# The last gelu of batch 1 ahead of the copies of batch 0's output, and T4's sums made beside batch 1's first product and stored

## The chip, the cores and the metric

The kernel runs on one core of one Trainium2 chip. The metric is device time in microseconds (us) of one execution; lower is better. A core has a matrix engine (PE, with its weight loads shown apart as PEld), a vector engine (DVE), a scalar engine for activations and copies (ACT), GpSimd (POOL, all but unused here) and a queue that issues the transfers between chip memory and HBM (SP). Each engine works through its own list of instructions in order, and waits where an instruction needs what another engine has not yet delivered.

## The reference

Eight batches, eight heads, 512 tokens and 32 states of width 64. Attention runs both ways between tokens and states; the 544 rows per batch then go through a two-layer network with the quick gelu.

```python
scores = scale * x @ state.T;   a  = softmax(scores);   xread = a  @ state      # 512 x 64 per head
scores2 = scale * state @ x.T;  a2 = softmax(scores2);  sread = a2 @ x          #  32 x 64 per head
y = concatenate([xread, sread], axis=2)          # rows of 512 features, heads side by side
h = y @ w_in                                     # 512 -> 2048
g = h * (1.0 / (1.0 + exp(-1.702 * h)))
return g @ w_out                                 # 2048 -> 512
```

All of it is in fp32.

## The kernel before, in words

**Tiles and batches.** The 512 tokens of a batch are four chunks of 128. The first product of the network is folded with the attention: for each batch, `att_M` multiplies the states with `w_in` (the tiles M), and the "up" product multiplies M with the transposed attention weights `aT`. Its gelu is written into tiles `g`, two of the 16 hidden chunks per tile. The second product, "down", multiplies the `g` tiles with `w_out`.

**Batches 0 and 1.** Batch 0 is done plainly: `up_x` (L529; its products are at L524, its gelu on ACT at L527) and `down` (L542), which adds the 16 hidden chunks into four PSUM banks, `bank_o[0]` to `bank_o[3]`, one for each chunk of tokens. The loop over f (from L1227 on) does one hidden chunk of batch 0's down product per step, and in its odd steps one of the last eight up products of batch 1, from the list `rest`. In the last step, f = 15, `down` also copies each bank into `osb` (L549, on ACT) and sends it out (L550, on SP); `osb` is one buffer, so each copy waits until the transfer of the one before has landed. In the source the last up product of batch 1 comes after these four copies, so its gelu stands behind them on ACT.

**Strassen.** From batch 1 on, products are done by Strassen's scheme (seven products in place of eight). The down product is `strassen_two`: the outer products P1 and P2 are plain (L745); the others, called P5, P6, P3, P7 and P4 in that order, are each done by a second level of seven small products, `strassen_low` (matmuls at L696; PSUM is gathered by DVE at L701 and copied by ACT at L705 and L711). The additions that prepare the left factors are DVE instructions (L752, of 0.68 us for 128x512). The right factors are sums of blocks of `w_out`, made once, around the end of the f loop: `T1`, `T2` and `T4` lie in `sums`, `T3` in `w_out`. Each of them needs three more sums for the inner level (`low_sums`, three subtractions of 128x512), and `low_third` (one subtraction in place). `low_made` puts the three sums in the tile `low`; `low_away` puts them in a room with the tag `xT` and stores them to HBM (`low_keep`, L648); later they are loaded from there (`low_load`, L645). The tag `xT` has one buffer: the next to use it is the exponentials of the next batch, `att_s_exp` (L372), which must wait until the store has read the room.

**T4.** Its sums are made in batch 1 by `low4_make`, as an entry of the hook `run`, between P3 and P7. They are written into the room with the tag `xn`, where batch 2's x lies until `att_sread` (L500 on PE) has read it. From batch 2 on `low4_load` (L666) loads them from HBM at the same place in the order. P4 is the first to read them.

**Order.** There is no scheduler: the order in the source is the order on each engine. What runs beside the products hangs on named hooks: "P1a" is called after the first half of P1, "P5.3" after the third small product of P5, "run" between P3 and P7. `hooks_next` fills them with the attention of the next batch. For batch 1 the entry "P1a" holds the last preparations of the right factors.

The end of the loop, where the change is made:

```python
        if f % 2 == 1:
            up_x(1, rest.pop(0))
        ...
        if f == NF - 1:
            for u in range(NU - 1):
                s3(1, u, S)
            T_of(B12, B22, B12)
            low_away(3, T3)
            low_third(T3)
            turn_x(2)
            low_made(2, T2, 0)
    s12(1, NU - 1, S)
    s3(1, NU - 1, S)
```

`s12` (L565, L566) and `s3` (L571) make left factors from the `g` tiles; the call for the last tile, `NU - 1`, needs the gelu of the last up product. `turn_x(2)` (L156) is four transposes, `low_made(2, T2, 0)` three subtractions into `low[:, 0:3]`, of which batch 1's `aT` is the first two thirds until the last up product has read it.

Of the kernel before, what the change touches and what calls it, by code (L numbers as in the profile page):

```python
# [20 lines left out]
def kernel(  # L21
# [39 lines left out]
    NF = DF // P  # L61
# [42 lines left out]
    T1, T2, T4 = (sums[:, i].rearrange("p (f n) -> p f n", f=HF) for i in range(3))  # L104
# [47 lines left out]
    def turn_x(b):  # L152

        A[b]["xT"] = xsq[b]
        for j in range(NPR):
            nc.vector.transpose(xsq[b][:, j], xsq[b][:, j])  # L156
# [36 lines left out]
    for i, v in enumerate((8.0 * most, 8.0 * (most - least))):  # L193
        t = konst.tile([P, 1], FP32, name=f"edge_{i}")
# [33 lines left out]
    def round_b(i, ahead, follows):  # L228


        if i not in begun:
            fraction(i)
        dst = begun.pop(i)
        lo, hi = words(i)
        sc = power.pop(i)
        nc.vector.scalar_tensor_tensor(sc, hi, -0x80000000, sc, ALU.bitwise_and, ALU.bitwise_or)
        powers_to(ahead)

        nc.vector.scalar_tensor_tensor(dst, lo, 2.0**-32, dst.bitcast(I32), ALU.mult, ALU.add)
        del raw[i]  # L240
        if follows and i + 1 in raw:
            fraction(i + 1)
        nc.vector.scalar_tensor_tensor(dst, dst, 2.0**-20, sc.bitcast(FP32), ALU.mult, ALU.mult)
# [3 lines left out]
    def before(i):  # L247

        nin = NFC * NPR
        return i - (nin - NPR if i < nin else 2 * NPR if i < nin + NPR else NPR)  # L250

    def load_weights(upto):
        while done["load"] < min(upto, len(PIECES)):
            load_weight(done["load"])
            done["load"] += 1

    def powers_to(n):
        while done["a"] < min(n, len(PIECES)):
            load_weights(done["a"] + 1)
            round_a(done["a"])  # L260
            done["a"] += 1

    def round_to(n, ahead=AHEAD):

        nin = NFC * NPR
        while done["b"] < min(n, len(PIECES)):
            i = done["b"]
            powers_to(i + 1)
            round_b(i, min(i + 1 + ahead, max(nin, i + 1)), i + 1 < nin and (i + 1 < n or i >= NPR))
            done["b"] += 1  # L270
            while done["b"] > NPR and done["load"] < len(PIECES) and before(done["load"]) < done["b"]:
                load_weights(done["load"] + 1)
# [209 lines left out]
    def att_eT(b, g):  # L482

        a = A[b]
        if g == 0:
            a["eT"] = apool.tile([P, NG, SCH, P], FP32, tag="eT", name=f"eT_{b}")
        ps = att_ps([P, SCH, P], f"eT_{b}_{g}")
        for c in range(SCH):
            nc.tensor.transpose(ps[:, c], a["e2"][g][0][:, P * c : P * (c + 1)], ident)
        nc.scalar.copy(a["eT"][:, g], ps)  # L490
# [29 lines left out]
    def up(key, f, ntok, lhs, rhs, spare=False):  # L520
        hps = att_ps([P, ntok], f"h_{key}_{f}") if spare else psH.tile([P, ntok], FP32, tag="h", name=f"h_{key}_{f}")
        n = len(lhs)
        for i in range(n):
            nc.tensor.matmul(hps, lhs[i], rhs[i], start=(i == 0), stop=(i == n - 1))  # L524
        if f % 2 == 0:
            G[key, f // 2] = free.pop(0)
        nc.scalar.activation(out=G[key, f // 2][:, f % 2, :ntok], in_=hps, func=AF.Gelu_apprx_sigmoid)  # L527

    def up_x(b, f, spare=False):  # L529
        c, o = divmod(P * f, FC)  # L530
        m = A[b]["M", c]
        up(b, f, S, [m[:, g, o : o + P] for g in range(NG)], [A[b]["aT"][:, g] for g in range(NG)], spare)
# [3 lines left out]
    def down(key, r, fs, dst, last):  # L536

        if fs[0] == 0:
            O[key, r] = bank_o[r]
        ops = O[key, r]  # L540
        for f in fs:
            nc.tensor.matmul(  # L542
                ops, G[key, f // 2][:, f % 2, P * r : P * (r + 1)], w_out[:, f], start=(f == 0), stop=(f == NF - 1)
            )
            if last and f < HF and f % 2:
                free.append(G.pop((key, f // 2)))
        if fs[-1] == NF - 1:
            osb = opool.tile([P, DM], FP32, tag="osb", name=f"osb_{key}_{r}")
            nc.scalar.copy(osb, ops)  # L549
            nc.sync.dma_start(dst, osb)  # L550
# [96 lines left out]
    def low_keep(k, src):  # L647
        nc.sync.dma_start(outside[k], src)  # L648

    def low4_room():  # L650
        t = xpool.tile([P, SCH, H, D], FP32, tag="xn", name="low4")
        return t.rearrange("p c h d -> p (c h d)")[:, : 3 * FC]

    def low_parts(t):
        return [t[:, FC * k : FC * (k + 1)].rearrange("p (f n) -> p f n", f=QF) for k in range(3)]

    def low4_make(a):
        t = low4_room()
        for fn, args in low_sums(T4, low_parts(t)):
            fn(*args)  # L660
        low_keep(4, t)
        a["low4"] = t

    def low4_load(a):
        a["low4"] = low4_room()
        nc.sync.dma_start(a["low4"], outside[4])  # L666
# [6 lines left out]
    def halves_of(t):  # L673

        return [t[:, QF * i : QF * (i + 1), P * k : P * (k + 1)] for i in range(2) for k in range(2)]

    def low_sums(t, rooms):

        b11, b12, b21, b22 = halves_of(t)
        t1, t2, t4 = rooms  # L680
        return [(T_of, v) for v in ((t1, b12, b11), (t2, b22, t1), (t4, b21, t2))]

    def low_third(t):
        _, b12, _, b22 = halves_of(t)
        T_of(b12, b22, b12)
# [441 lines left out]
    def rounds(n):  # L1127
        round_to(done["b"] + n)
# [78 lines left out]
    B11, B12, B21, B22 = (w_out[:, HF * i : HF * (i + 1), HN * k : HN * (k + 1)] for i in range(2) for k in range(2))  # L1207

    def T_of(t, x0, x1):
        nc.vector.tensor_tensor(out=t, in0=x0, in1=x1, op=ALU.subtract)  # L1210
# [15 lines left out]
    rest = list(range(2 * nper, NF))  # L1226
    for f in range(NF):  # L1227
        rounds(1)
        round_to(NFC * NPR + f + 1)
        for r in range(SCH):  # L1230
            down(0, r, [f], out_x[0, r], r == SCH - 1)
        if f in (0, 2):
            for g in range(NG):
                att_eT(f // 2, g)
        if f in (0, nper * 2):
            att_M(1, 2 + f // (nper * 2))
        if f in (1, 3):
            att_sread(f // 2)
        if f in (2, 4):
            att_srT(f // 2 - 1)  # L1240
        if f % 2 == 1:
            up_x(1, rest.pop(0))
        if f == HF:
            load_state(2)
            load_x_squares(2)
        if f == NF - 2:
            T_of(T1, B12, B11)
            low_away(6, B22)
            low_made(5, T1, 1)
            for u in range(NU - 1):  # L1250
                s12(1, u, S)
            T_of(T2, B22, T1)
            low_third(T1)
        if f == NF - 1:
            for u in range(NU - 1):
                s3(1, u, S)
            T_of(B12, B22, B12)
            low_away(3, T3)
            low_third(T3)
            turn_x(2)  # L1260
            low_made(2, T2, 0)
    s12(1, NU - 1, S)
# [5 lines left out]
    for b in range(1, B):  # L1268
        if b > 1:
            ahead = {"P1a": [(up_strassen(b, S, *parts_x(b), A[b]["sums"]), ())]}  # L1270
        else:
            ahead = {"P1a": [(low_third, (B22,)), (T_of, (T4, B21, T2)), (low_third, (T2,))], "P7.7": [(low_third, (T4,))]}
        if b + 1 < B:
            if b > 1:
                turn_x(b + 1)
            hooks = hooks_next(b + 1)
        else:

            steps, left, right = sr_sums()
            order = (  # L1280
                ("P5.6", 2), ("P6.1", 3), ("P6.3", 6), ("P6.4", 7), ("P7.5", 8), ("P7.6", 9), ("P4.1", 16, 17), ("P4.5", 18, 19),
            )
            hooks = {name: [steps[i] for i in n] for name, *n in order}
            hooks["P3.7"] = [(low_third, (T1,))]
            beside = steps[10:16] + [(low_third, (t,)) for t in (T2, T3, T4, B22)]
            ahead["P1a"][:0] = [steps[i] for i in (0, 1, 4, 5)]
        for name, first in ahead.items():
            hooks[name] = first + hooks.get(name, [])
        a4 = {}

        at = hooks.setdefault("run", [])
        k = 3 if b + 1 < B else 0
        at[k:k] = [(low4_load if b > 1 else low4_make, (a4,))]
        strassen_two(b, out_of(b), hooks, a4)
        if b + 2 < B:
            load_state(b + 2)
            load_x_squares(b + 2)
# [35 lines left out]
```

## Time and profile before

Three runs took 713.96, 714.00 and 714.05 us. The profiled execution is one of 713.74 us, of which the engines' span is 712.0 us; its granted PE clock is 0.998.

| engine | busy us | share of the span | instructions |
|---|---|---|---|
| PE | 697.9 | 98% | 4973 |
| DVE | 602.0 | 85% | 1246 |
| ACT | 231.2 | 32% | 456 |
| POOL | 0.8 | 0% | 8 |

The transfers moved 77.1 MB, 108 GB/s over the span. Shares of busy time are means over stages with different limits. What a change in one stage is worth is read from that stage's timeline and waits: which engine stands still, and for whom. In the trace the stage around the change runs from about 144 us (the f loop's last two steps) to 209.4 us (the first up product of batch 2); batch 2's same stage, from P1 on, ends at 285.1 us.

### The profile page before, as it was taken

To read this page: it belongs to the slowest core of one execution; us is meant where nothing else is said; L and a number is where in the kernel's file an instruction comes from. 1 tells how busy PE (TensorE), PEld (TensorE's weight loads), DVE (VectorE), ACT (ScalarE), POOL (GpSimd) and SP (SyncE) were. 2 spreads that over 40 slices of the span, in tenths; PEclk is the share of its full clock that TensorE was granted. 3 is DMA by queue.
4 is the path that set the end of the run, shared out by engine and by line. 5 is a ranking of instruction groups with operands and counts; after the bars stand their busy time and mean duration, and the time that the engine had idled before them with its cause. 6 is when DMAs were issued, how large, how long until landed. Compare 5 with 4: busy or idle time off the path is not lost.

```text
span 712.0 us, 12663 instructions
## 1 busy us (share of the span) xinstructions
PE 697.9 (98%) x4973; PEld 557.9 (78%) x4975; DVE 602.0 (85%) x1246; ACT 231.2 (32%) x456; POOL 0.8 (0%) x8
## 2 busy tenths in 40 slices
PE   8989999999999999999999999999999999999996
PEld 3433444457888799888998899879987998899995
DVE  6999899969988999789968997899789997888650
ACT  5686511023214322433233322441343224300210
POOL 0000000000000000000000000000000000000000
PEclk9999999999999999999999999999999999999999
DMA  8921246217633184408550674138431940031001
GB/s 234 363 78 53 95 150 138 115 45 188 190 128 61 34 202 144 87 0 182 164 118 1 117 202 119 29 71 192 141 60 34 203 145 22 0 114 66 16 1 29
DMA packets 143770, 77.10 MB, mean 108 GB/s; under 512 B 113888, under 2 KB 127712, under 8 KB 143712
## 3 DMA queue, kind: packets, MB, share of 16 engines
q1 hardware_dynamic: 143712, 76.31, 41.1%
q8 instruction: 39, 0.64, 0.4%
q14 instruction: 19, 0.16, 0.1%
HBM read 60.29 MB, written 15.99 MB: 107 GB/s over the span
## 4 chain that ended last, share of the span: by engine, by line
PE 93%; ACT 2%; DVE 2%; DMA 2%; SPq 0%; issue 0%; DVEq 0%; ACTq 0%
PE low L696 21%; PE o L1058 17%; PE o L745 14%; PE o L696 10%; PE o L542 8%; PE h L524 7%; PE upx L1058 6%; PE M L320 4%; PE o L585 2%; PE o L320 1%; PE sr L500 1%; PE warm L125 1%; PE upx_sr L1058 1%; DMA out_dram<-osb_sr 1%; DMA xn<-in_x_dram 1%; DVE g L752 1%
## 5 line engine op out<-in xcount | busy, mean ns | idle before, releaser
L1068 DVE TENSOR_TENSOR g<-o,g 128x512 f32<-128x512 f32 (+1 forms) x140 | 88.0, 650 | 51.1 <-PE o L1058 50.2
L745 PE MATMUL o<-w_out,g 128*128 128x256 f32 x448 | 100.5, 380 | 0.0
L745 PEld LDWEIGHTS o<-w_out,g 128*128 128x128 f32 x448 | 84.2, 190 | 16.9 <-issue 5.5
L1065 ACT ACTIVATE g<-g 128x512 f32<-128x512 f32 (+1 forms) x84 | 49.8, 600 | 100.8 <-DVE g L1068 100.8
L1058 PE MATMUL upx<-aT,M 128*128 128x256 f32 x192 | 49.3, 379 | 0.0
L1058 PE MATMUL o<-ta,M 128*128 128x256 f32 x192 | 49.3, 379 | 0.0
L1058 PE MATMUL o<-ta,ms 128*128 128x256 f32 x192 | 48.3, 379 | 0.0
L696 PE MATMUL low<-low,g 128*128 128x128 f32 x336 | 44.4, 275 | 0.0
L460 ACT COPY M<-M 128x512 f32<-128x512 f32 x64 | 33.2, 596 | 28.1 <-PE M L320 28.1
L696 PEld LDWEIGHTS low<-low,g 128*128 128x128 f32 x336 | 40.9, 192 | 0.0
L1058 PEld LDWEIGHTS o<-ta,ms 128*128 128x128 f32 x192 | 36.5, 190 | 5.0
L1058 PEld LDWEIGHTS o<-ta,M 128*128 128x128 f32 x192 | 36.5, 190 | 5.0
L1058 PEld LDWEIGHTS upx<-aT,M 128*128 128x128 f32 x192 | 36.0, 190 | 4.7
L696 PE MATMUL low<-sums,later 128*128 128x128 f32 x280 | 37.1, 275 | 0.0
L696 PEld LDWEIGHTS low<-sums,later 128*128 128x128 f32 x280 | 34.6, 192 | 0.5 <-ACT pu L705 0.2
L320 PE MATMUL M<-w_in,stT 64*32 64x512 f32 x512 | 32.7, 594 | 0.2 <-ACT eT L490 0.2
L524 PE MATMUL h<-low,M 128*128 128x512 f32 x64 | 29.8, 600 | 1.4 <-DVE low L408 1.4
L696 PE MATMUL low<-w_out,g 128*128 128x128 f32 x224 | 29.7, 275 | 0.9 <-DVE pu L701 0.9
L524 PE MATMUL h<-aT,M 128*128 128x512 f32 x64 | 28.7, 599 | 1.4 <-ACT M L460 1.4
L542 PE MATMUL o<-w_out,g 128*128 128x512 f32 x64 | 28.7, 594 | 0.0
L542 PE MATMUL o<-w_out,sums 128*128 128x512 f32 x64 | 28.4, 594 | 0.0
L696 PEld LDWEIGHTS low<-w_out,g 128*128 128x128 f32 x224 | 27.3, 192 | 1.1 <-DVE pu L701 1.1
(208 smaller groups left out, 1282.2 us busy)
## 6 DMA issues: line engine op xcount, KB each, us to landing
low<-low SPq DMA_DIRECT2D x78, 256.0 KB, 3.6
later<-in_moe_w_out_dram SPq DMA_DIRECT2D x16, 512.0 KB, 3.4
xn<-in_x_dram SPq DMA_DIRECT2D x28, 256.0 KB, 4.8
low<-low SPq DMA_DIRECT2D x9, 768.0 KB, 4.6
w_out<-in_moe_w_in_dram SPq DMA_DIRECT2D x12, 512.0 KB
xsq<-in_x_dram SPq DMA_DIRECT2D x96, 64.0 KB, 2.3
out_dram<-osb SPq DMA_DIRECT2D x18, 256.0 KB, 3.0
out_dram<-later SPq DMA_DIRECT2D x14, 256.0 KB, 2.2
```

What stands on the lines that cost most here:

```text
L125: nc.tensor.matmul(ps, zeros[:, :P], zeros, start=True, stop=True)
L320: nc.tensor.matmul(ps[g][st], A[b]["stT"][rows, st], rhs(rows, j), start=True, stop=True)
L460: nc.scalar.copy(m[:, g], ps[g])
L500: nc.tensor.matmul(ps[st, g], a["eT"][:, g, c, st], xn[b][:, c, NG * j + g], start=(c == 0), stop=(c == SCH - 1),)
L524: nc.tensor.matmul(hps, lhs[i], rhs[i], start=(i == 0), stop=(i == n - 1))
L542: nc.tensor.matmul(ops, G[key, f // 2][:, f % 2, P * r : P * (r + 1)], w_out[:, f], start=(f == 0), stop=(f == NF - 1))
L585: nc.tensor.matmul(ps[:, r], lhs[f][:, P * r : P * (r + 1)], rhs[:, f], start=(first and r == 0 and f == 0), stop=(f == HF - 1), skip_grou ...
L696: nc.tensor.matmul(ps, lhs[f], rhs[:, f], start=(first and f == 0), stop=(f == QF - 1), skip_group_check=True)
L745: nc.tensor.matmul(ps[:, r], lhs[f][:, P * r : P * (r + 1)], rhs[:, f], start=(r == 0 and f == 0), stop=(f == HF - 1), skip_group_check=True,)
L1058: nc.tensor.matmul(ps[:, k], lhs[i][:, o : o + P], rhs[i], start=(first and k == 0 and i == 0), stop=(i == n - 1), skip_group_check=True,)
L1065: nc.scalar.activation(out=dst, in_=src, func=AF.Gelu_apprx_sigmoid)
L1068: nc.vector.tensor_tensor(out=dst, in0=ps, in1=x, op=ALU.add)
```

## The change

Three things, all around the seam between batch 0 and batch 1:

1. The last up product of batch 1 comes at the head of step f = 15, ahead of batch 0's last down products, their copies and their output transfers.
2. The preparations with `s3`, `T3` and its `low_away` move from step 15 into step 14, ahead of the output transfers in the source. On DVE the order of these instructions stays what it was; on SP the store of T3's sums now stands ahead of the four output transfers.
3. `low4_make` goes away. T4's three sums are made by `low_away(4, T4)` in the hook "P1a" of batch 1, in the `xT` room, and are stored; `low_third(T4)` follows them there, and leaves "P7.7". In "run" batch 1 now loads the sums from HBM as the other batches do.

```diff
-    def low4_make(a):
-        t = low4_room()
-        for fn, args in low_sums(T4, low_parts(t)):
-            fn(*args)
-        low_keep(4, t)
-        a["low4"] = t
...
         round_to(NFC * NPR + f + 1)
+        if f == NF - 1:
+
+            up_x(1, rest.pop(0))
         for r in range(SCH):
             down(0, r, [f], out_x[0, r], r == SCH - 1)
...
-        if f % 2 == 1:
+        if f % 2 == 1 and rest:
             up_x(1, rest.pop(0))
...
             T_of(T2, B22, T1)
             low_third(T1)
-        if f == NF - 1:
             for u in range(NU - 1):
                 s3(1, u, S)
             T_of(B12, B22, B12)
             low_away(3, T3)
             low_third(T3)
+        if f == NF - 1:
             turn_x(2)
             low_made(2, T2, 0)
...
-            ahead = {"P1a": [(low_third, (B22,)), (T_of, (T4, B21, T2)), (low_third, (T2,))], "P7.7": [(low_third, (T4,))]}
+            ahead = {
+                "P1a": [(low_third, (B22,)), (T_of, (T4, B21, T2)), (low_third, (T2,)), (low_away, (4, T4)), (low_third, (T4,))]
+            }
...
-        at[k:k] = [(low4_load if b > 1 else low4_make, (a4,))]
+        at[k:k] = [(low4_load, (a4,))]
```

## The prediction

> **What bounds the kernel now.** First the chain that ended last:
>
> ```profile
> PE 93%; ACT 2%; DVE 2%; DMA 2%; SPq 0%; issue 0%; DVEq 0%; ACTq 0%
> ```
>
> PE carries the end. An edit that adds no matmul and removes none can only win time in which PE stands still, so the second view is PE's waits over the whole span. Leaving out the first 100 us, four rows remain, and all four lie in batch 1's second product:
>
> ```profile
> PE low L696 <- DVE pu L701: 0.9, 1, 0.9
> ...
> PE low L696 <- DVE later L701: 0.4, 1, 0.4
> PE low L696 <- ACT M L460: 0.4, 1, 0.4
> ...
> PE o L696 <- DVE spare_M L701: 0.3, 1, 0.3
> ```
>
> That is 2.0 us of plain idleness, but matmuls that trickle also cost, so I compare stage lengths. The third view is busy time by stage: first batch 1 (inner products of P5; then from the sread matmuls to the end of P4), below it the same two stages of batch 2. Columns: window, length, busy us of PE, PEld, DVE, ACT, POOL with counts, clock, DMA share, GB/s.
>
> ```profile
> 171.55:178.65 7.10, 6.83 (x57) 6.46 (x56) 6.93 (x19) 2.61 (x7) 0.00 (x0) 1.00 0.68 106
> 191.37:209.43 18.06, 16.39 (x211) 14.47 (x211) 16.31 (x42) 3.81 (x11) 0.00 (x0) 1.00 0.40 130
> 250.46:256.71 6.25, 6.25 (x57) 6.25 (x56) 6.00 (x16) 1.62 (x5) 0.00 (x0) 1.00 0.85 140
> 269.42:285.05 15.63, 15.63 (x211) 14.25 (x210) 13.93 (x38) 3.81 (x11) 0.00 (x0) 1.00 0.50 150
> ```
>
> The PE work is the same, yet batch 1 takes 0.85 and 2.43 us longer: **3.28 us** in all. Between them P6 and P3 take 12.72 against 12.71. Batch 2 has no PE wait at all, so 3.28 us is the most these stages can give. DVE is nearly full in batch 1 (6.93 of 7.10): DVE is late there. Why, the timelines of ACT and of DVE tell (start, length, instruction, idle before it and its releaser):
>
> ```profile
> 158.81 0.59 ACT L549 COPY osb<-o 128x512 f32<-128x512 f32 x1 [2.15 <-DMA out_dram<-osb]
> 159.29 0.60 ACT L527 ACTIVATE g<-h 128x512 f32<-128x512 f32 x1
> ```
>
> ```profile
> 154.03 0.69 DVE L1210 TENSOR_TENSOR low<-sums 128x512 f32<-128x512 f32 x1 [1.40 <-PE h L524]
> 154.89 1.42 DVE L1210 TENSOR_TENSOR low<-sums,low 128x512 f32<-128x512 f32 x2 [0.17 <-PE h L524]
> 159.93 0.69 DVE L565 TENSOR_TENSOR later<-g,g 128x512 f32<-128x512 f32 x1 [3.62 <-ACT g L527]
> ...
> 192.53 0.69 DVE L1210 TENSOR_TENSOR low<-sums 128x512 f32<-128x512 f32 x1 [0.77 <-PE sr L500]
> 193.26 1.42 DVE L1210 TENSOR_TENSOR low<-sums,low 128x512 f32<-128x512 f32 x2
> 194.59 0.75 DVE L752 TENSOR_TENSOR later<-g,g 128x256 f32<-128x256 f32 x2
> ```
>
> The last gelu's product is finished at about 154.7, but the gelu runs at 159.29, behind four copies that wait for each other's transfers. DVE idles 3.62 us for it, and 1.40 + 0.17 before that for the last up product. After 159.93 DVE runs without a gap to 191.8, and then spends 2.83 us (191.76 to 194.59) on T4's sums, of which 0.77 is a wait.
>
> [...] T3's sums are done on DVE at 149.6, and their store, behind the output transfers on SP, issues at 159.85. [...]
>
> **The change part by part.**
>
> *Gelu ahead.* On PE the up product (1.72 us) trades places with the down products of f = 15 (3.43 us, half of the last 6.87); the sum is unchanged. It ends at about 151.3 in place of 154.7, and the gelu at 152.0. Then DVE no longer idles: `turn_x` ends at 152.63, the three sums of T2 follow until 154.7, and the last `s12` starts there: 1.40 + 0.17 + 3.62 = 5.19 us earlier. T4 itself needs the last down products, done at 154.7; DVE reaches it at about 157.3, so no wait.
>
> *Copies later.* The four `osb` copies move by 1.72 us, to 152.3 … 160.5 (ends 161.1). P1 reuses the first bank at 154.69, and the first copy ends at 152.9. P2 takes the second bank at 161.7, copied by 155.6. The scores at 165.26 need the last banks (161.1) and the state's transpose copied by ACT behind them (161.4). The copy of P1 follows on ACT at about 161.8, as now (162.04). Cost: nothing, hidden behind P1.
>
> *T4's sums beside P1.* Three subtractions take 2.05 us from start to next start (as 132.34 to 134.39), and `low_third(T4)` 0.62 (164.78 to 165.40): 2.67 us more on DVE. So the sums for P5 start at 165.40 − 5.19 + 2.67 = 162.88, a lead of 2.52 us. The scores' transposes would start at 167.09, after PE's scores (166.35). The gathering of P2, at 173.70 now, could start at 171.18 and is held by PE until 171.7: 0.2 us after P5 begins. In batch 2 it starts 0.77 us after (251.23 against 250.46) with no PE wait. Hence P5's **0.85 us** goes. ACT's exponentials start when the table is loaded, 169.37 + 1.28 = 170.65, and take 1.5 us, so ACT is free before P5's first copy, as in batch 2.
>
> *T4's sums out of "run".* DVE gets 2.83 us back, and its next step starts 0.4 us after the sread matmuls start (3.22 − 2.83); in batch 2 it is 0.32. Hence **2.43 us** goes. The wait booked on ACT's M copy goes too: in batch 2 the copies end at the same distance with no wait, and the real releaser is DVE's `later`, a left factor. `low_third(T4)` leaving P7.7 frees 0.60 us of DVE where it then idles: nothing.
>
> *Transfers.* T3's store issues at 149.7, not 159.85, and has landed (3.3 us on the `away` rows) before T4's sums want the room. On SP the order is then: four outputs (last issued at 161.2), T2's store, T4's store at about 162.4, batch 2's x at 166.63 as now. T4's store lands at 165.7 to 167.1 (3.3 to 4.7 us, the two ends of the store rows), before ACT's table load at 169.37: the new wait of the exponentials for the room costs 0, with 2 us to spare; above it can cost what the slower rival says, and it cannot gain. T4's load is in batch 2's row: issued 1.16 us after sread starts, landed after 4.4, first read 10.3 after (279.69): hidden. Behind it on SP is only T2's load, which waits for P7 (274.41 in batch 2).
>
> Sum: 0.85 + 2.43 = 3.28; 712.0 − 3.3 = 708.7 of span. The stages behind P4 stand to each other as in batch 2 (DVE's last step 0.59 us after the next up product's start in both), so nothing gives it back. The runs lie 2.0 us above the span: **714.0 − 3.3 = 710.7**.
>
> **The rivals.**
>
> - *Half of it*: P5's stall stays, because DVE's lead is eaten by waits that this trace does not show (T4's sums are new where they stand). Only 2.43 us: 711.6. Between this and 713 any part may be lost.
> - *No change*: it is not the gelu that holds DVE, so the lead is 0. Then 2.67 us of T4's sums fall on P5 and 2.43 come back in "run": 714.2. Against it stands the releaser at 159.93, which fits ACT's timeline. Also here: the time is taken back in batch 2's stages; but there DVE waits for PE, not PE for DVE.
> - *Slower*: T4's store holds the `xT` room, and the exponentials wait, with P5's first copy behind them on ACT. Exponentials at 171.71 are what the kernel has now, at 0.85 us of stall; later ones stop PE one for one. It turns into a loss if the store lands after 171.7 + 2.4 = 174.1, that is 11.7 us after issue; the slowest row of transfers now takes 8.9. With a landing at 176 it gives 716. For it: three transfers leave SP within 2 us there. Against: 2 us of slack and a DMA share of 0.58 in 150 to 180.
>
> **How the numbers follow.** Forecast 0.76, half 0.13, no change 0.07, slower 0.04. The forecast's own spread is 710.3 to 711.1; the range goes up to 712.0 to take in half of the gain, and down to 710.2, since PE has nothing else to win there. A measurement can tell about 0.2% (1.4 us) from no change. Faster by more: forecast and half, 0.88 with a little lost between; same 0.08; slower 0.04.
>
> **What would show it.** Right: the last gelu near 151.5, DVE's 3.62 and 1.40 idle gone, P5's inner products in 6.25 us, sread to P4 in 15.63, no PE wait at L696, T3's store near 149.7, T4's landed before ACT's table load. Wrong: a table load or an exponential that waits for a transfer, a P5 over 6.5 us, or a new PE wait at P1 or P2.

## The result, and the profile after

The changed kernel takes 710.56 us (four runs, 710.48 to 710.89) against 713.98 for the kernel before beside it (713.92 to 714.05): a ratio of 0.9953, 95% interval 0.9936 to 0.9970. That is 3.4 us, where 3.3 were forecast. The interval, 2.1 to 4.6 us, would by itself also hold the 2.43 us of the rival "half of it"; the stage lengths below decide between the two. The span of the profiled execution falls from 712.0 to 708.8 us.

First the chain that ended last, and the first and last rows of PE's waits over the whole span:

```profile
PE 95%; ACT 2%; DMA 2%; SPq 0%; DVE 0%; issue 0%; DVEq 0%; ACTq 0%
```

```profile
PE h L524 <- DVE low L408: 1.4, 1, 1.4
...
PE srT L514 <- ACT eT L490: 0.3, 1, 0.3
PE M L320 <- ACT eT L490: 0.2, 1, 0.2
```

DVE's 2% of the chain have become PE's. No wait at the inner products (L696 before, L689 now) is left; every row that remains lies in the first 100 us. Then the busy time by stage, as before: P5's inner products, P6 and P3, and from the sread matmuls to the end of P4 (columns: window, length, busy us of PE, PEld, DVE, ACT, POOL, clock, DMA share, GB/s).

```profile
171.69:177.94 6.25, 6.25 (x58) 6.25 (x56) 5.28 (x14) 1.62 (x5) 0.00 (x0) 1.00 0.82 138
177.94:190.66 12.72, 12.72 (x115) 12.60 (x113) 12.51 (x33) 1.69 (x5) 0.00 (x0) 1.00 0.77 215
190.66:206.28 15.62, 15.62 (x210) 14.24 (x210) 13.94 (x38) 3.81 (x11) 0.00 (x0) 1.00 0.48 150
```

The lengths 7.10, 12.72 and 18.06 have become 6.25, 12.72 and 15.62: 0.85 and 2.44 us are gone, and PE is busy in each stage from end to end. P5 begins 0.14 us later than before (171.69 against 171.55); PE was as much later already ahead of the change's place (143.67 against 143.53 for the same down product). 3.29 − 0.14 is the 3.2 us of the spans. The way there, on ACT, on DVE and on SP:

```profile
151.60 0.60 ACT L527 ACTIVATE g<-h 128x512 f32<-128x512 f32 x1 [4.55 <-PE h L524]
152.45 0.59 ACT L549 COPY osb<-o 128x512 f32<-128x512 f32 x1 [0.26 <-PE o L542]
...
160.81 0.59 ACT L549 COPY osb<-o 128x512 f32<-128x512 f32 x1 [2.25 <-DMA out_dram<-osb]
...
169.50 1.28 ACT L372 ACT_TABLE_LOAD   x1
```

```profile
154.58 0.69 DVE L565 TENSOR_TENSOR later<-g,g 128x512 f32<-128x512 f32 x1
...
160.04 0.69 DVE L1203 TENSOR_TENSOR away<-sums 128x512 f32<-128x512 f32 x1
...
162.70 0.68 DVE L745 TENSOR_TENSOR spare_M<-later 128x512 f32<-128x512 f32 x1
...
171.94 0.69 DVE L745 TENSOR_TENSOR osb<-o,g 128x512 f32<-128x512 f32 x1 [0.86 <-DMA xn<-in_x_dram]
```

```profile
149.59 0.32 SPq L648 DMA_DIRECT2D low<-away  x1
153.06 8.69 SPq L550 DMA_DIRECT2D out_dram<-osb  x4
161.85 0.38 SPq L648 DMA_DIRECT2D low<-low  x1
162.32 0.40 SPq L648 DMA_DIRECT2D low<-away  x1
```

The last gelu runs at 151.60 (159.29 before), the last left factors on DVE start at 154.58 with no wait (159.93), T4's sums at 160.04, and the sums for P5 at 162.70 (165.40). DVE then reaches P2's sum early and waits 0.86 us for it; the row names batch 2's x, which this instruction does not read, and in e4 below the same wait, there of 0.83 us, is put down to PE's P2, whose sums it does read. T3's store leaves at 149.59 (159.85), T4's at 162.32. ACT's table load, ahead of the exponentials that take T4's room, starts without a wait right behind the M copies.

### The profile page after: what moved, and what is told of

It reads as the page before. It is cut to its first block, busy times and chain, and to the rows that moved or that the text cites. A ratio compares the mean times of both kernels' runs of the same rounds, so it can differ in the third digit from the quotient of the medians.

```text
span 708.8 us, 12669 instructions
## 1 busy us (share of the span) xinstructions
PE 696.3 (98%) x4975; PEld 557.4 (79%) x4975; DVE 602.7 (85%) x1246; ACT 231.2 (33%) x456; POOL 0.8 (0%) x8
## 4 chain that ended last, share of the span: by engine, by line
PE 95%; ACT 2%; DMA 2%; SPq 0%; DVE 0%; issue 0%; DVEq 0%; ACTq 0%
PE low L689 21%; PE o L1051 17%; PE o L738 14%; PE o L689 10%; PE o L542 8%; PE h L524 7%; PE upx L1051 6%; PE M L320 4%; PE o L585 2%; PE o L320 1%; PE sr L500 1%; PE warm L125 1%; PE upx_sr L1051 1%; DMA out_dram<-osb_sr 1%; DMA xn<-in_x_dram 1%; ACT low L219 1%
## 5 line engine op out<-in xcount | busy, mean ns | idle before, releaser
L689 PE MATMUL low<-low,g 128*128 128x128 f32 x336 | 44.4, 275 | 0.0
L689 PEld LDWEIGHTS low<-low,g 128*128 128x128 f32 x336 | 40.9, 192 | 0.0
L689 PE MATMUL low<-sums,later 128*128 128x128 f32 x280 | 37.0, 275 | 0.0
L689 PEld LDWEIGHTS low<-sums,later 128*128 128x128 f32 x280 | 34.6, 192 | 0.4
L689 PE MATMUL low<-w_out,g 128*128 128x128 f32 x224 | 29.6, 275 | 0.0
L527 ACT ACTIVATE g<-h 128x512 f32<-128x512 f32 x24 | 14.0, 591 | 45.1 <-PE h L524 45.1
```

Of the source, the lines that this page charges most:

```text
L689: nc.tensor.matmul(ps, lhs[f], rhs[:, f], start=(first and f == 0), stop=(f == QF - 1), skip_group_check=True)
```

## The experiments

Each was timed beside the kernel before, whose median there lay between 713.88 and 713.98 us; the ratio is to that. e1 and e2 are edits of the kernel before, the others of the changed kernel. "P5" is the time from the first inner product of P5 to the first of P6, "sread to P4" the last of the three stages.

| kernel | time, us | ratio, 95% interval | P5, us | sread to P4, us |
|---|---|---|---|---|
| before | 713.98 | | 7.10 | 18.06 |
| changed | 710.56 | 0.9953 (0.9936 to 0.9970) | 6.25 | 15.62 |
| e1, gelu ahead only | 713.03 | 0.9988 (0.9981 to 0.9994) | 6.25 | 18.07 |
| e2, T4's sums only | 715.03 | 1.0013 (1.0006 to 1.0019) | 9.78 | 15.62 |
| e3, T3's store late | 714.81 | 1.0007 (0.9999 to 1.0016) | 10.52 | 15.63 |
| e4, four more stores | 718.97 | 1.0070 (1.0057 to 1.0083) | 14.69 | 15.63 |
| e5, one more store | 710.43 | 0.9951 (0.9938 to 0.9965) | 6.25 | 15.62 |
| e6, four more subtractions | 710.88 | 0.9959 (0.9947 to 0.9972) | 6.25 | 15.63 |
| e8, seven more | 712.08 | 0.9975 (0.9965 to 0.9985) | 7.86 | 15.62 |
| e7, ten more | 714.24 | 1.0006 (0.9998 to 1.0014) | 9.71 | 15.62 |

### The two halves of the change, each alone

e1, the last gelu ahead, on the kernel before:

```diff
+        if f == NF - 1:
+            up_x(1, rest.pop(0))
         for r in range(SCH):
             down(0, r, [f], out_x[0, r], r == SCH - 1)
...
-        if f % 2 == 1:
+        if f % 2 == 1 and rest:
```

> The kernel before with one edit: the last up product of batch 1 stands ahead of batch 0's last down products (T4's sums stay in 'run', the T3 block stays in step 15). Theory (two separate DVE delays, each worth its own PE stall): DVE's idle 3.62 and 1.40 us are gone, P5's inner products take 6.25 us in place of 7.10, the stage from sread to the end of P4 stays near 18.06 us, since T4's sums there wait for sread whatever DVE's lead. Gain 0.85 us: 713.1. Rival 1 (the lead lasts into 'run'): the second stage shortens too and the gain is 2 us or more, 712.0 or less. Rival 2 (DVE was not held by this gelu): 714.0.

Measured 713.03 us, 0.89 less than the 713.92 beside it. Its stages P5 and sread to P4:

```profile
171.58:177.83 6.25, 6.25 (x58) 6.25 (x56) 5.28 (x14) 1.61 (x5) 0.00 (x0) 1.00 0.81 131
...
190.55:208.62 18.07, 16.39 (x210) 14.47 (x210) 16.32 (x42) 3.81 (x11) 0.00 (x0) 1.00 0.42 130
```

The gelu is worth P5's stall and nothing more. DVE's lead does not last into "run", since T4's sums there start with a wait for sread: it is 0.77 us in e1, as before, and PE's waits behind it are the same three of 0.9, 0.4 and 0.4 us.

e2, T4's sums in "P1a" and loaded in "run", on the kernel before:

```diff
-            ahead = {"P1a": [(low_third, (B22,)), (T_of, (T4, B21, T2)), (low_third, (T2,))], "P7.7": [(low_third, (T4,))]}
+            ahead = {"P1a": [..., (low_third, (T2,)), (low_away, (4, T4)), (low_third, (T4,))]}
...
-        at[k:k] = [(low4_load if b > 1 else low4_make, (a4,))]
+        at[k:k] = [(low4_load, (a4,))]
```

> The kernel before with the other edit alone: T4's sums made in 'P1a' in the xT room, stored, and loaded in 'run'; the last gelu stays behind the copies. Theory: the stage from sread to the end of P4 falls from 18.06 to 15.63 us (-2.43), but the 2.67 us of T4's sums now land on DVE ahead of P5 with no lead to pay for them: P5 grows from 7.10 to about 9.8 us. Sum +0.24: 714.2, no gain. Rival (P5's stall comes from ACT or PE and not from DVE's lateness): P5 stays at 7.1 us and the gain is 2.4 us, 711.6.

The stages came out as expected, 9.78 and 15.62 us. The time is 715.03, not 714.2. The 21 executions fall into two groups: six with a mean clock of 0.999 at 713.98 to 714.41, fifteen with 0.997 or less at 714.84 to 716.29. The profiled one, at 713.98, is of the first group; what the second group pays is told with e3. PE's waits, and ACT in the same stage:

```profile
PE low L696 <- ACT pu L705: 2.7, 1, 2.7
PE o L696 <- DVE spare_M L701: 0.3, 1, 0.3
```

```profile
172.11 1.28 ACT L372 ACT_TABLE_LOAD   x1 [2.79 <-DMA low<-away]
174.37 0.69 ACT L372 ACTIVATE e<-o,mx 128x512 f32<-128x512 f32 x1 [0.97 <-DVE mx L359]
...
175.83 0.26 ACT L705 COPY pu<-low 128x128 f32<-128x128 f32 x1
```

PE waits for ACT's copy, and the copy stands behind the exponentials. What these wait for last is DVE's maximum (0.97 us). The table load ahead of them had waited for T4's store (2.79 us, from the M copies on), but was through in time, at 173.39. So DVE is the cause, though PE's row names ACT. Without the gelu's lead T4's sums cost P5 slightly more (2.68 us) than they free behind sread (2.44 us). `low_third(T4)` left "P7.7" together with the sums, but it had held nothing: PE's last wait in that stage of the kernel before ends at 201.28, and `low_third(T4)` starts at 203.62. The two halves alone change the time by −0.9 us and, at full clock, by about +0.1; together they change it by −3.4. One pays for the other.

### The store that was moved along

e3 is the changed kernel with the T3 block back in step 15:

```diff
             low_third(T1)
+        if f == NF - 1:
             for u in range(NU - 1):
                 s3(1, u, S)
             T_of(B12, B22, B12)
             low_away(3, T3)
             low_third(T3)
-        if f == NF - 1:
             turn_x(2)
```

> The changed kernel with only the T3 block (s3, T3, its sums and their store) put back into step 15, so that on SP the store stands behind the four output transfers again; DVE's order is the same. Theory (the move of the store is needed): the store issues at about 162, lands at about 165.3, and T4's sums, which take the same room, wait for it from 160.0 on: 5.3 us of DVE. P5 starts 2.6 us later on DVE than in the kernel before and takes about 9.7 us; the stage after sread keeps 15.63. Time 714.1 to 714.3: the whole gain is gone. Rival (the place of this store costs nothing): 710.6.

DVE has the same list as in the changed kernel, and waits at the first of T4's sums:

```profile
165.61 0.69 DVE L1203 TENSOR_TENSOR away<-sums 128x512 f32<-128x512 f32 x1 [4.87 <-DMA low<-away]
```

The whole gain is gone: five executions at 713.78 to 714.15 with a clock of 0.999, eight at 714.76 to 715.28 with 0.997 or less. The profiled one is of the second group. PE in P5, and the granted clock by stage:

```profile
176.36 1.42 PE L689 MATMUL low<-sums,later 128*128 128x128 f32 x8 [2.38 <-ACT pu L698]
177.57 1.92 PE L689 MATMUL o<-low,spare_M 128*128 128x128 f32 x8
179.28 1.66 PE L689 MATMUL low<-sums,later 128*128 128x128 f32 x8
180.78 1.06 PE L689 MATMUL o<-sums,spare_M 128*128 128x128 f32 x8
```

```profile
177.00:178.00 1.00, 1.00 (x8) 1.00 (x6) 1.00 (x4) 0.51 (x2) 0.00 (x0) 0.56 0.42 66
178.00:180.00 2.00, 2.00 (x11) 2.00 (x11) 1.83 (x5) 0.08 (x1) 0.00 (x0) 0.50 0.97 143
180.00:181.00 1.00, 1.00 (x9) 1.00 (x8) 0.44 (x2) 0.00 (x0) 0.00 (x0) 0.73 0.95 145
```

After an idle stretch of 2.38 us PE's granted clock was 0.56, 0.50 and 0.73 in these three windows and 1.00 again in 182 to 184 us, and eight matmuls took up to 1.92 us in place of 1.06. As an estimate, with the shares 0.56 and 0.73 taken as made up of 1.00 and 0.50, half the clock was granted from 177.1 to 180.5, that is for 3.4 us. P5 lost 1.03 us by it (worked out below), and the medians of e3's two groups lie 1.0 us apart. Of the second groups of e2 and e7 no trace was kept; their lower mean clock, mostly 0.997, would fit the same estimate, since 3.4 us at half clock in 713 us lower the mean by 0.0024.

### How long the T4 store may take

e4 and e5 add four stores or one of the same room to other places in HBM, behind the first:

```diff
         low_keep(k, room)
+        if k == 4:
+            for i in range(4):
+                nc.sync.dma_start(more[i], room)
```

> The changed kernel with four more stores of T4's sums to other places in HBM (4 x 768 KB more traffic) right behind the first, so that the xT room comes free later. Theory (the exponentials' wait for the room sits on ACT's table load, which has about 3 us to spare): the last store lands at about 174.5 in place of 167, the table load then starts there in place of 169.5, P5's first copy on ACT follows some 3 us later at 177.5, and PE, which needs it at 173.5, stands still about 4 us: 714.6, with P5 at about 10 us. Rival (nothing waits for the store of T4, the room is free without it): 710.6.

> The changed kernel with one more store of T4's sums to another place in HBM (768 KB more traffic) right behind the first. Theory (the exponentials' wait for the room has 2 to 3 us to spare): five stores held the table load until 176.2, so one store more is some 2.3 to 2.8 us; the room then comes free at about 169.5, just when ACT comes to its table load, and PE loses nothing: 710.6, P5 in 6.25 us. Rival (the slack is used up already): P5 longer by up to 2.5 us, 713.

ACT's table load in e4, then in e5:

```profile
176.19 1.28 ACT L372 ACT_TABLE_LOAD   x1 [6.84 <-DMA more<-away]
```

```profile
169.99 1.28 ACT L372 ACT_TABLE_LOAD   x1 [0.55 <-DMA more<-away]
```

So the new wait is there, and the table load carries it. With one more store it lasts 0.55 us and costs nothing: P5 stays at 6.25 us and the time at 710.43. With four more PE stands still 5.64 us and then runs at half clock (0.50 in 178 to 184 us), for 8.4 us in all, not the 4 expected: the room came free 1.7 us later than I had reckoned, and the slow clock adds some 2.6 us (three groups of eight matmuls whose starts lie 1.86, 1.71 and 1.70 us apart in place of 0.89).

### How much DVE slack P5 has

e6, e8 and e7 put four, seven or ten subtractions of 128x256 more on DVE, behind `low_third(T4)`:

```diff
-                "P1a": [..., (low_away, (4, T4)), (low_third, (T4,))]
+                "P1a": [..., (low_away, (4, T4)), (low_third, (T4,))]
+                + [(T_of, (pu.rearrange("p k n -> p (k n)"), T4[:, 0], T4[:, 1]))] * 4
```

> The changed kernel with four subtractions of 128x256 more on DVE after T4's third (into pu, which is free then): 1.4 to 1.6 us of DVE, nothing else. Theory (P5 needs DVE at P2's sum no later than about 0.8 us after P5 begins, as in batch 2): DVE comes to it about 0.9 us after, PE loses 0 to 0.2 us: 710.6 to 710.8. Rival (every microsecond of DVE ahead of P5 costs PE one): 712.0.

> The same with ten such subtractions, 3.4 to 3.8 us of DVE. Theory: the slack of about 1.5 us is used up and the rest stops PE one for one: DVE comes to P2's sum about 3 us after P5 begins (2.15 us in the kernel before, where P5 lost 0.85), P5 loses 1.7 to 2.1 us: 712.3 to 712.7. Rival (the loss in P5 is not one for one, as DVE catches up inside P5): 711.9 or less.

> The changed kernel with seven subtractions of 128x256 more on DVE after T4's third, about 3.1 us (the ten took 4.5). It tests a line drawn through four traces: with L the time from P5's begin to DVE's sum of P2, PE loses in P5 L - 1.30 us (L 1.16: 0; 2.15: 0.85; 4.76: 3.46; 4.82: 3.53). Theory: L is about 2.6 us (1.16 with four subtractions, plus three at 0.45), P5 takes 7.5 us and the time is 711.8. Rival (the loss has a step, so that PE loses 2 us or more as soon as ACT's exponentials come late): P5 8.3 us or more, 712.6. [...]

DVE's sum of P2 (`osb`), the instruction by which its lateness was judged, in the kernel before, e2, e6, e8 and e7:

```profile
173.70 0.68 DVE L752 TENSOR_TENSOR osb<-o,g 128x512 f32<-128x512 f32 x1
```

```profile
176.35 0.68 DVE L752 TENSOR_TENSOR osb<-o,g 128x512 f32<-128x512 f32 x1
```

```profile
172.80 0.68 DVE L745 TENSOR_TENSOR osb<-o,g 128x512 f32<-128x512 f32 x1
```

```profile
174.62 0.69 DVE L745 TENSOR_TENSOR osb<-o,g 128x512 f32<-128x512 f32 x1
```

```profile
176.49 0.69 DVE L745 TENSOR_TENSOR osb<-o,g 128x512 f32<-128x512 f32 x1
```

P5 begins at 171.55, 171.53, 171.64, 171.71 and 171.73. With L the lateness of this sum after P5's begin, and the loss P5's length less 6.25 us:

| | L, us | loss in P5, us | L − loss |
|---|---|---|---|
| changed (DVE waits for PE there) | 0.25 | 0 | |
| batch 2, before | 0.77 | 0 | |
| e6 | 1.16 | 0 | |
| before | 2.15 | 0.85 | 1.30 |
| e8 | 2.91 | 1.61 | 1.30 |
| e7 | 4.76 | 3.46 | 1.30 |
| e2 | 4.82 | 3.53 | 1.29 |

The four rows with a loss lie on one line, L less 1.30 us (1.29 in e2). As an estimate from them, DVE may come up to 1.30 us late here, and from there on PE loses one for one; no run has an L between 1.16 and 2.15. e6 lies below that limit: its P5 takes 6.25 us, its span (708.7 us) is that of the changed kernel, and its rival, a loss from the first microsecond on, is out. e8 was expected from this line before it ran. Its L became 2.9 and not 2.6 (the seven subtractions took 3.18 us, 0.45 each, and DVE came to T4's sums 0.4 us later than in e6), and its time was 712.08 and not 711.8, with nine runs from 711.98 to 712.39; the step of its rival is not there. e7 missed its expectation (712.3 to 712.7) by the same two things: ten subtractions took 4.5 us and not 3.4 to 3.8, and DVE came to T4's sums 0.9 us later than in the changed kernel. At full clock its runs lie at 713.67 to 714.43. e3, left out of the table, has L 4.54; the line gives 3.24 us and P5 lost 4.27. The 1.03 us more go with the half clock, under which groups of eight took up to 1.92 us in place of 1.06.

The 0.9 us come from ahead of the edit. In e7 DVE waits for the last load of `w_out`, which leaves SP behind the sixteen transfers of batch 2's x:

```profile
127.42 0.43 DVE L207 TENSOR_SCALAR low<-later 128x512 int32<-128x512 int32 x1 [0.81 <-DMA later<-in_moe_w_out_dram]
```

The same wait is 0.28 us in e8, 0.18 in e3 and 0.16 in the kernel before, and the changed kernel's trace has none, though none of these edits is near it. Such a delay takes from DVE's slack in P5, 0.9 us in e7, though no edit stands near it.

None of the runs points to a kernel faster than the changed one: in this stage PE has no idle time left to win.

## Why the prediction was right, by its steps

- **The size from the stage lengths.** 0.85 + 2.43 us was read off against batch 2, as the most that the two stages could give; the trace after has 0.85 + 2.44. The four named waits alone would have promised 2.0 us. The rest was matmuls that trickled: around P5's wait groups of eight start 0.95 to 1.05 us apart in place of 0.89.
- **The time from the span.** "2.0 us above the span" set the median of the runs, 714.0, against the span of an execution of 713.74 us. The executions of both kernels lie about 1.8 us above their own spans. The forecast is a difference, so this slip did not touch it.
- **The gelu.** "5.19 us earlier" became 5.35 (159.93 to 154.58). ACT kept to the order of its list: the gelu at 151.60 ahead of the first copy at 152.45, where before it came at 159.29, behind the last one at 158.81. e1 shows its worth alone: P5's stall.
- **T4's sums beside P1.** 2.67 us of DVE were forecast, 2.66 measured (160.04 to 162.70), and the start of P5's sums at 162.88 became 162.70. DVE comes to P2's sum 0.25 us after P5's begin (0.2 forecast). With the 0.86 us that DVE waits there, 1.05 more up to the limit of 1.30 make 1.9 us to spare, and e6 spent 1.8 of them without a loss; batch 2 had only shown that 0.77 is harmless.
- **T4's sums out of "run".** e2 shows that 2.44 us come back there even where P5 is late, so the two stages are separate accounts.
- **The wait put down to ACT's M copy.** It was taken for DVE's left factor. It is gone after the change, and it stays in e1, where T4's sums stay in "run".
- **The transfers.** T3's early store was named as landed before T4's sums want its room. e3 shows that this is a condition and not a detail: without it the whole gain is lost. That the room's wait costs nothing is shown by e5, where a whole store more still costs nothing.
- **The rivals.** "Half of it" is the size of neither part alone: what P5 alone gives (e1) is a quarter, and the other part alone gives nothing (e2). "No change", with no lead, was worked out as 714.2; e2 is that case, and at full clock it has 713.98 to 714.41. The slower rival has its mechanism right (e4) and its price wrong in two terms: it left out that the table load, 1.28 us, comes after the landing, and its "one for one" left out the slower clock, 2.6 us. Together that is more than the 3.0 us by which e4 lies above its 716, so one for one was itself somewhat too much where only ACT is late. As an estimate from e4's chain, 2.96 us from the table load's start to PE's next product, and that product's start at 173.47 in the changed kernel, the loss begins when the table load is held beyond about 170.5.

How early the single T4 store really lands in the changed kernel is not shown by a wait, since nothing waits for it. In e2 and e3 the table load was released 4.56 and 4.54 us after the issue of T4's store, and in e3 DVE 3.55 us after that of T3's. The same from 162.32 would be 165.9 to 166.9, an estimate, at least 2.6 us ahead of the table load.

## What to carry to other kernels

Where PE carries the chain, compare a stage's length with the same stage of a later, undisturbed batch: where PE has no idle time in that batch, the difference is the most that an edit which leaves PE's work alone can win there, and it includes the trickle that the wait rows leave out. When two edits meet on one engine that does its list in order, as DVE did here (in e3 T4's sums and P5's sums behind them both came 5.57 us later, the latter at 168.27 in place of 162.70), sum their effects by the moment at which PE needs that engine, not by each edit's own gain: here −0.9 and about +0.1 made −3.4, since one made the slack that the other spent. And a buffer with a single room carries its store with it: an edit that writes there sooner must bring the store ahead of it in the queue too (in e3 T3's store left SP at 162.06, behind the outputs, in place of 149.59, and T4's sums waited 4.87 us for it).

## What the runs showed of the hardware that was not expected

In e3 and e4 an idle stretch of PE cost more than itself. In e3's profiled execution one of 2.38 us was followed by half the clock (0.50 in 178 to 180 us; 3.4 us of it by the estimate above) and one microsecond of loss. The estimate puts the begin of the half clock at 177.1, some 0.8 us after PE had started again. In e4's, with a stretch of 5.64 us up to 179.15, it lasted twice as long: by the same working, from 0.83 of the clock in 177 to 178 us and 0.75 in 184 to 185, an estimate of 177.7 to 184.5. In e2's profiled execution a stretch of 2.67 us was not followed by a lower clock (1.00 in each window from 168 to 190 us), nor was one of 2.58 us in e7's (1.00 over P5).

Over all timed runs of e2, e3 and e7 28 of 47 executions show a mean clock of 0.997 or less, and their medians lie 1.0, 1.0 and 0.7 us above those of the others of their kernel. In e7 the two groups all but touch (714.43 and 714.56). In e8, whose profiled execution has no stretch above 0.74 us in this stage, the nine runs keep together within 0.4 us, though one of them, the longest, also shows 0.997. In e4 (5.64 us in the profiled one) all five have 0.995 or less.

What decides whether an execution gets the half clock is not shown: executions of one kernel fall on both sides by their mean clock, and 2.38 us was followed by it where 2.58 and 2.67 us were not. How short a stretch can still bring it was not tried either. In the kernel before one of 1.45 us, ended at 37.49, left the clock at 1.00 in 30 to 40 and in 40 to 60 us; what a stretch between that and 2.38 us does is not shown.
